# A pooled-attention and gated-MLP kernel on one core: its opening rebuilt

## The chip, the core and the metric

The kernel runs on one core of one Trainium2 chip. A core has five engines that run their own instruction queues and wait for each other through semaphores: PE (TensorE, matrix products into PSUM), DVE (VectorE), ACT (ScalarE), POOL (GpSimd) and SP (SyncE, which here only issues transfers). Transfers between main memory and the on-chip SBUF run on 16 DMA engines. The metric is the device time of one execution in microseconds (us).

## The reference

Eight batches of 576 positions; eight heads of 64. Keys and values are averaged over groups of 8 positions (72 pooled keys a head), then softmax attention, then a gated MLP whose gate mixes positions by the matrix `w_sg`.

```python
k_p = k.reshape(B, H, 72, 8, 64).mean(axis=3)          # the same for v_p
scores = 0.125 * q @ k_p.T                             # 576 x 72 for each head
attn = exp(scores - max); attn /= attn.sum() + 1e-9
x = concat_heads(attn @ v_p)                           # 8 x 576 x 512
h = gelu_tanh(x @ w_in)                                # w_in 512 x 1024
u, v = h[..., :512], h[..., 512:]
v_n = (v - mean) / sqrt(var + 1e-6) * g_ln
v_s = einsum('ts,bsd->btd', w_sg, v_n) + b_sg
out = x + (u * v_s) @ w_out                            # w_out 512 x 512
```

`w_in` and `w_out` arrive as 64-bit floats (4 MB and 2 MB), everything else as 32-bit floats.

## The kernel before

**Data.** A product in full precision is made of three products of rounded operands: every operand is split into a rounded part (`...h`, `...hi`) and a rest (`...l`, `...lo`), and high x high, high x low and low x high are summed in PSUM. For batch 0 alone (`WHOLE = (0,)`) the attention's value products run on unsplit 32-bit operands; each such product leaves two records on PE.

**Steps.** The work of one batch `b` is cut into steps, written as generators that advance piece by piece. A, B, C, E load keys, values, queries and the "left" rows (the last 8 of the 72 pooled rows of each head, kept apart); K pools the keys and writes the block-diagonal `kbd`; P pools the values; Q brings the queries of a head pair into `qT` (head dimension on partitions); S computes scores, their negated maximum `nmax`, the exponentials `e`, their sums `ssum`, and normalises; L and T transpose `e` (its left columns `el`, and the rest); V multiplies by the values and splits the result into `xhl`; H makes one row block of the value half of `w_in` (then gelu and the layer norm); U one column block of the other half; W multiplies by `w_sg`, gates; O multiplies by `w_out`; Z stores. Lower-case names are for weights: `lv0`, `lv1` load the two halves of `w_in`'s value columns, `lu0`, `lu1` the other columns, `lo0`, `lo1` `w_out`, `ls0` `w_sg`; `v0`..`v3`, `u0`..`u3`, `o0`..`o3` convert one piece of 128 x 512 numbers from 64 bits to two 32-bit parts (`step_w`); `s0`..`s4` transpose `w_sg`.

**Order.** Nothing is scheduled by a tool: two written tables set the order. `PROLOGUE` is the opening, a list of names such as `V0+0` (step V of head pair 0, batch 0) or `S0+1` (batch 1); each mention advances that step by one piece. `PERIOD` is repeated for each later batch. At the end every instruction is tied to the one before it on its engine, so each engine's queue runs exactly in the written order, and an instruction that waits holds all that stands behind it. All loads stand on SP's queue and share this rule: a load into a tile that is still being read waits, and so do the loads behind it.

**What the change touches.** In `load_q` the queries of every batch are loaded as 32-element runs, four transfers for a head pair, and `step_Q` turns them on DVE (L419). In `step_w`, ACT scales the high word (L198), DVE rebuilds sign and exponent (L201, L202) and takes the power of two apart (L203), ACT converts the low word to a number (L206) and rounds the high part (L207), POOL multiplies, subtracts and adds (L209, L219, L220). `BY_PSUM` makes the `v` pieces pass through PSUM. In `step_P`, batch 0's left values are scaled in place in the tile `left` (rows 64 to 96, L387); `step_V` multiplies those 32 rows (`lt[64:96]`) as a product of its own. `step_S` makes 10 exponentials a head pair (L453), each with its own bias and an accumulated sum. PSUM is used as two rings of two tiles, `mps` (MLP, weights and batch 0's scores) and `aps` (attention).

Of the kernel before, what the change touches and what calls it, by code (L numbers as in the profile page):

```python
# [35 lines left out]
O0+0 O1+0 S0+2 S1+2 O1+0 S2+2 O1+0 P2+2 V1+1 S2+2 C3+2 V3+1 S1+2 O2+0 O2+0 Z0+0 O2+0 V1+1 H2+1 S1+2 T0+2 S2+2
H2+1 S0+2 Q3+2 Z0+0 Z1+0
""".split()
PERIOD = """
# [11 lines left out]
def tile_pooled_attn_gmlp(ctx: ExitStack, tc: tile.TileContext, q, k, v, w_in, g_ln, w_sg, b_sg, w_out, out):  # L51
# [19 lines left out]
    BY_SUM = ()  # L71
# [79 lines left out]
    def load(o, i, queue=nc.sync):  # L151
        queue.dma_start(o, i)  # L152
# [593 lines left out]
```

## Time and profile before

| | us |
|---|---|
| median of the runs | 606.53 (603.07 to 606.60, 3 runs) |
| span of the profiled execution | 608.8 |
| PE's first product / first product of `w_sg` (step W) | 5.78 / 121.27 |
| one period of the repeated part | 66.0 |

For the profiled execution the record gives its span, 608.8 us, and no time of its own beside it; it is 2.3 us above the median of the runs. A row of a timeline reads: start, duration, engine, line, operation, output <- inputs, shape, how often in a row, and in brackets how long the engine had been idle and what ended it. The table by stretches gives for each engine its busy time and number of instructions, then PE's granted clock (1.00 is full speed), the busy share of the DMA engines and GB/s.

### The profile page before, as it was taken

How to read it: one execution, taken by the hardware profiler on the slowest of the kernel's cores; microseconds unless marked ns; L12 is line 12 of the kernel's file. 1: busy time of each engine (PE TensorE's matmuls, PEld its weight loads, DVE VectorE, ACT ScalarE, POOL GpSimd, SP SyncE). 2: the span in 40 equal slices, each digit the busy share in tenths (PEclk: the TensorE clock that was granted, in tenths of full speed). 3: DMA queues.
4: the chain of work that ended last, by engine and by line, in shares of the span. 5: the costliest groups of instructions: out<-in, count | busy, mean ns of one | idle time of the engine just before them, and what ended most of it. 6: DMA issues, size and time to landing. Idle time of an engine off the chain costs nothing.

```text
span 608.8 us, 10393 instructions
## 1 busy us (share of the span) xinstructions
PE 569.4 (94%) x3769; PEld 529.3 (87%) x3769; DVE 410.8 (67%) x566; ACT 360.8 (59%) x1091; POOL 235.5 (39%) x304
## 2 busy tenths in 40 slices
PE   3579569899999999999999999999999999999996
PEld 3564258899989998999999998999899999999996
DVE  1663698887785878667876878587866866434444
ACT  1685677957855677549754775567755975422310
POOL 2515756658240613253242523161324323242320
PEclk9575788999999999999999999999999999999999
DMA  7897460415325153413343162515341210112104
GB/s 173 185 271 199 101 165 4 88 36 95 59 55 110 36 106 64 92 36 79 54 92 75 37 112 55 110 36 102 67 92 19 40 21 1 20 25 34 20 1 78
DMA packets 166018, 46.33 MB, mean 76 GB/s; under 512 B 153488, under 2 KB 153488, under 8 KB 165968
## 3 DMA queue, kind: packets, MB, share of 16 engines
q1 hardware_dynamic: 161200, 45.10, 34.8%
q10 hardware_dynamic: 4768, 0.59, 0.6%
q8 instruction: 29, 0.48, 0.3%
q14 instruction: 21, 0.17, 0.1%
HBM read 36.23 MB, written 9.44 MB: 75 GB/s over the span
## 4 chain that ended last, share of the span: by engine, by line
PE 87%; ACT 5%; DVE 3%; DMA 2%; SPq 1%; issue 1%; POOL 0%; DVEq 0%; ACTq 0%; POOLq 0%
PE mps L97 68%; PE aps L97 13%; PE aps L134 4%; ACT e L453 3%; DMA raw<-in_moe_w_in 1%; SPq L152 1%; PE mps L242 1%; DVE top L202 1%; DMA left<-in_v 1%; DVE nmax L436 0%; DVE e L464 0%; PE aps L348 0%; DVE ssum L460 0%; ACT u L604 0%; POOL top L219 0%
## 5 line engine op out<-in xcount | busy, mean ns | idle before, releaser
L97 PE MATMUL mps<-wih,xhl 128*128 128x512 f32 x256 | 87.3, 407 | 4.6 <-ACT vg L567 4.6
L97 PE MATMUL mps<-xhl,wih 128*128 128x288 f32 x512 | 90.0, 298 | 0.7 <-DVE vg L563 0.7
L453 ACT ACTIVATE e<-aps,nmax 128x72 f32<-128x72 f32 x280 | 85.5, 353 | 4.1 <-DVE nmax L436 3.8
L629 POOL TENSOR_TENSOR glo<-u,ghi 128x576 fp32r<-128x576 f32 x32 | 45.3, 1427 | 108.1 <-ACT ghi L627 107.2
L97 PEld LDWEIGHTS mps<-xhl,wih 128*128 128x128 f32 x512 | 75.8, 189 | 2.4 <-DVE vg L563 1.0
L453 ACT ACTIVATION_READ_ACCUMULATOR e<-aps,nmax 128x1 f32 x280 | 66.8, 239 | 0.0
L97 PEld LDWEIGHTS mps<-wih,xhl 128*128 128x128 f32 x256 | 49.2, 192 | 16.1 <-ACT vg L567 5.0
L618 DVE SCALAR_TENSOR_TENSOR mps<-mps,gcol,bbc 128x576 f32<-128x576 f32 x32 | 26.4, 825 | 52.2 <-PE mps L97 52.2
L574 POOL TENSOR_TENSOR rstd<-mv,eps 128x1 f32<-128x1 f32 (+1 forms) x40 | 10.6, 264 | 117.4 <-DVE mv L572 107.9
L97 PE MATMUL mps<-wsh,vhh 128*128 128x288 f32 x256 | 55.7, 299 | 0.0
L97 PE MATMUL mps<-wsh,vhl 128*128 128x288 f32 x256 | 55.2, 297 | 0.0
L97 PE MATMUL mps<-xhl,wil 128*128 128x288 f32 x256 | 55.0, 296 | 0.0
L577 DVE TENSOR_SCALAR vg<-vg,mv,rstd 128x512 f32<-128x512 f32 (+1 forms) x40 | 41.6, 1041 | 19.8 <-POOL rstd L575 19.7
L97 PE MATMUL mps<-wsl,vhh 128*128 128x288 f32 x256 | 54.8, 295 | 0.0
L534 POOL TENSOR_TENSOR xhl<-x,xhl 128x576 fp32r<-128x576 f32 x32 | 45.3, 1430 | 22.4 <-ACT xhl L528 22.4
L97 PE MATMUL mps<-ghi,woh 128*128 128x288 f32 x240 | 52.6, 300 | 0.0
L97 PE MATMUL mps<-wil,xhl 128*128 128x512 f32 x128 | 51.5, 402 | 0.0
L97 PE MATMUL mps<-glo,woh 128*128 128x288 f32 x240 | 51.3, 295 | 0.0
L97 PE MATMUL mps<-ghi,wol 128*128 128x288 f32 x240 | 51.3, 295 | 0.0
L567 ACT ACTIVATE vg<-mps 128x512 f32<-128x512 f32 x32 | 19.0, 599 | 50.1 <-PE mps L97 49.9
L587 POOL TENSOR_TENSOR vhl<-vg,vhh 128x512 fp32r<-128x512 f32 x32 | 42.5, 1330 | 9.7 <-ACT vhh L585 9.6
L627 ACT CAST ghi<-u 128x576 fp32r<-128x576 f32 x32 | 21.5, 674 | 38.0 <-DVE u L620 38.0
(146 smaller groups left out, 1454.0 us busy)
## 6 DMA issues: line engine op xcount, KB each, us to landing
qraw<-in_q SPq DMA_DIRECT2D x128, 72.0 KB
out<-y SPq DMA_DIRECT2D x118, 72.0 KB
kvraw<-in_k SPq DMA_DIRECT2D x32, 256.0 KB
kvraw<-in_v SPq DMA_DIRECT2D x32, 256.0 KB
raw<-in_moe_w_in SPq DMA_DIRECT2D x4, 1024.0 KB
raw<-in_moe_w_out SPq DMA_DIRECT2D x2, 1024.0 KB
stage<-in_moe_w_sg SPq DMA_DIRECT2D x4, 288.0 KB
left<-in_k SPq DMA_DIRECT2D x16, 64.0 KB
```

The source lines that it names most:

```text
L97: nc.tensor.matmul(o, lhsT, rhs, start=start, stop=stop)
L134: nc.tensor.transpose(ps[:rows, i * P:(i + 1) * P], src(i), ident if i < NT - 1 else swap)
L152: queue.dma_start(o, i)
L453: nc.scalar.activation(e[:, i, h], slots[i][:, h], AF.Exp, bias=nmax[:, i, h:h + 1], **acc)
L534: nc.gpsimd.tensor_tensor(xhl[:, 1, g], x32[:, g], xhl[:, 0, g].bitcast(F32), op=ALU.subtract)
L567: nc.scalar.activation(vg, o, AF.Gelu_apprx_tanh)
L574: nc.gpsimd.tensor_tensor(rstd, mv[:, 1:2], eps[:n, 1:2], op=ALU.add)
L577: nc.vector.tensor_scalar(vg, vg, mv[:, 0:1], rstd, op0=ALU.subtract, op1=ALU.mult)
L587: (nc.gpsimd if i < NT - 1 else nc.vector).tensor_tensor(lo, vg, hi.bitcast(F32), op=ALU.subtract)
L618: nc.vector.scalar_tensor_tensor(vs, vs, gcol[:, d:d + 1], bbc.rearrange("p (a n) -> p a n", a=2), op0=ALU.mult, op1=ALU.add)
L627: nc.scalar.copy(ghi[:, d], uf)
L629: nc.gpsimd.tensor_tensor(glo[:, d], uf, ghi[:, d].bitcast(F32), op=ALU.subtract)
```

## The change

`PERIOD` is the same list with other line breaks. `PROLOGUE` is a new list with the same work, and these parts of the program are changed:

- **Queries of batch 0** (`NATURAL = (0,)`): two transfers a head pair with runs of 64 elements, into one large tile `early` (head pairs 0 to 2; it also takes batch 0's values) and a fourth buffer, so that no load of them waits for a reader. PE transposes them, six products of 128 x 96 a head pair, and ACT copies the result to `qT`.
- **Value products of batch 0**: `vl` and `lt` are tiles of their own with 96 rows, 64 of them zeroed at the start by POOL; step V multiplies all 96. `left` is no longer read by step V. `ah` alternates between two buffers.
- **Weights**: the low word, scaled, is added as an integer to the rebuilt high word (one POOL addition in place of a DVE mask, a POOL product and a POOL addition); rounding and rest follow. The pieces no longer pass through PSUM.
- **Softmax** of head pairs 1 and 3 of batch 0 and all four of batch 1 (`SOFTMAX`): DVE subtracts the maximum, ACT makes one exponential of 128 x 720, DVE sums.
- **Step H of batch 0**: all products with `xhl`'s high part first, the four with its low part last.
- **Loads of `w_in`'s value half** are issued on POOL's queue.

```diff
-    NATURAL = ()
+    NATURAL = (0,)
+    Q_ACT = (0, 1, 2, 3)
-    BY_PSUM = ("v",)
+    BY_PSUM = ()
-    SOFTMAX = {}
+    SOFTMAX = ((0, 1), (0, 3), (1, 0), (1, 1), (1, 2), (1, 3))
+    W_POOL = ("v",)
...
+    early = per.tile([P, 4 * POOL * D + 18 * P], F32, name="early", tag="xhl")
...
-        load(raw, sv)
+        load(raw, sv, nc.gpsimd if name in W_POOL else nc.sync)
...
             nc.scalar.activation(bits.bitcast(F32), high.bitcast(F32), AF.Copy, scale=2.0 ** -112)
-            yield
-            x = ring(per, shape, "vg", 3)
+            nc.scalar.activation(low, low.bitcast(U32), AF.Copy, scale=2.0 ** -29)
+            yield
             nc.vector.tensor_scalar(bits, bits, 3, None, op0=ALU.logical_shift_left)
             nc.vector.scalar_tensor_tensor(top, high, -0x80000000, bits, op0=ALU.bitwise_and, op1=ALU.bitwise_or)
-            nc.vector.tensor_scalar(x.bitcast(I32), top, -0x800000, None, op0=ALU.bitwise_and)
+            yield
+            nc.gpsimd.tensor_tensor(top, top, low, op=ALU.add)
+            yield
             top = top.bitcast(F32)
-            yield
-            nc.scalar.activation(low.bitcast(F32), low.bitcast(U32), AF.Copy, scale=2.0 ** -52)
             nc.scalar.copy(hi, top)
             yield
-            nc.gpsimd.tensor_tensor(x, x, low.bitcast(F32), op=ALU.mult)
...
-                nc.gpsimd.tensor_tensor(top, top, hi.bitcast(F32), op=ALU.subtract)
-                nc.gpsimd.tensor_tensor(lo, x, top, op=ALU.add)
+            (nc.vector if name in LO_W else nc.gpsimd).tensor_tensor(lo, top, hi.bitcast(F32), op=ALU.subtract)
...
+            for h in range(2):
+                load(t[:, :, h], q[b, 2 * g + h].rearrange("(t p) d -> p t d", t=6))
...
+        st["vl", b] = per.tile([96, 2, 4, D], F32, name="vl", tag="vl")
+        nc.gpsimd.memset(st["vl", b][0:64], 0.0)
+        for gp in range(2):
+            st["lt", b, gp] = per.tile([96, S], F32, name="lt", tag=f"lt{gp}")
+            nc.gpsimd.memset(st["lt", b, gp][0:64], 0.0)
...
+            ps = (mtile if g < 2 else atile)()
             for i in range(6):
+                nc.tensor.transpose(ps[:, i // 3, n * (i % 3):n * (i % 3 + 1)],
+                                    t[:, i].rearrange("p h d -> p (h d)"), ident[:n, :n])
+            yield
+            (nc.scalar.copy if g in Q_ACT else nc.vector.tensor_copy)(
+                qT.rearrange("p (a n) -> p a n", a=2), ps[:, :, 0:HALF])
...
-        mode = SOFTMAX.get(b, 0)
+        mode = 2 if (b, g) in SOFTMAX else 0
...
-                mm(o, vl[:, g // 2, gl:gl + 2], lt[64:96, sl], False, True)
+                mm(o, vl[:, g // 2, gl:gl + 2], lt[:, sl], False, True)
...
+        for c in range(KC if i < NT - 1 else 0):
+            mm(o, xhi[:, c, t], wih[:, c, sl], c == 0, False)
+            mm(o, xhi[:, c, t], wil[:, c, sl], False, False)
+            if b > 0:
+                mm(o, xlo[:, c, t], wih[:, c, sl], False, c == KC - 1)
         for c in range(KC):
             if i < NT - 1:
-                mm(o, xhi[:, c, t], wih[:, c, sl], c == 0, False)
-                mm(o, xhi[:, c, t], wil[:, c, sl], False, False)
-                mm(o, xlo[:, c, t], wih[:, c, sl], False, c == KC - 1)
+                if b == 0:
+                    mm(o, xlo[:, c, t], wih[:, c, sl], False, c == KC - 1)
```

**The loads on SP's queue**, from batch 0's last keys on. Before, as they stand in the queue (`kvraw`, `left`, `qraw` are keys and values, left rows and queries; `stage` is `w_sg`; `raw` are weights in 64 bits):

```order
L152 DMA stage<-in_moe_w_sg 64x576
L152 DMA bbc<-in_moe_b_sg 128x576
L152 DMA gcol<-in_moe_g_ln 128x4x1
L152 DMA qraw<-in_q 32x18x32 x4
L152 DMA raw<-in_moe_w_out 128x4x512
L152 DMA raw<-in_moe_w_in 128x4x512
L152 DMA kvraw<-in_k 64x2x512 x2
L152 DMA qraw<-in_q 32x18x32 x4
L152 DMA kvraw<-in_v 64x2x512 x2
L152 DMA raw<-in_moe_w_in 128x4x512
L152 DMA left<-in_k 32x1x512 x2
L152 DMA left<-in_v 32x1x512 x2
```

And now:

```order
L153 DMA stage<-in_moe_w_sg 64x576
L153 DMA bbc<-in_moe_b_sg 128x576
L153 DMA gcol<-in_moe_g_ln 128x4x1
L153 DMA kvraw<-in_k 64x2x512 x2
L153 DMA left<-in_k 32x1x512 x2
L153 DMA left<-in_v 32x1x512 x2
L153 DMA kvraw<-in_v 64x2x512 x2
L153 DMA raw<-in_moe_w_in 128x4x512
L153 DMA qraw<-in_q 32x18x32 x4
```

Batch 1's remaining keys and its left rows moved to directly behind `w_sg`, ahead of batch 1's values and queries and of three weight loads; the value half of `w_in` is gone from this queue.

**PE, the end of batch 0's attention**, from the second half of step V (`vb`, `ah`: values and transposed weights; `left`, `lt`: the left rows; `el`, `e`: exponentials; `kp`, `lp`: pooled keys). Before, with buffer numbers:

```order
L97 MATMUL aps_508<-ah_491,vb_106 128x288
L97 MATMUL aps_508<-lt_389,left_111 128x288
L242 MATMUL mps_520<-ident_70,stage_285 128x128
L242 MATMUL mps_520<-ident_70,stage_287 128x128
L242 MATMUL mps_520<-ident_70,stage_289 128x128
L242 MATMUL mps_520<-ident_70,stage_291 128x128
L242 MATMUL mps_520<-ident_70,stage_293 128x64
L348 MATMUL aps_540<-ident_70,kp_433 128x128 x2
L350 MATMUL aps_540<-ident_70,lp_93 128x128
L97 MATMUL aps_567<-kbd_84,qT_407 128x144 x5
L97 MATMUL aps_573<-kbd_84,qT_498 128x144 x5
L97 MATMUL mps_604<-wih_95,xhl_413 128x512
```

And now, from batch 1's keys on (each V step's two rows stand twice):

```order
L334 MATMUL aps_482<-ident_70,kp_304 128x128 x2
L336 MATMUL aps_482<-ident_70,lp_93 128x128
L99 MATMUL aps_500<-ah_466,vb_107 128x288
L99 MATMUL aps_500<-lt_113,vl_109 128x288
...
L99 MATMUL aps_511<-ah_475,vb_107 128x288
L99 MATMUL aps_511<-lt_113,vl_109 128x288
...
L99 MATMUL aps_518<-kbd_84,qT_488 128x144 x5
L99 MATMUL aps_545<-kbd_84,qT_506 128x144 x5
```

The key transposes of batch 1 moved from behind all four V steps to ahead of the last two, and two transposes of `w_sg` moved to ahead of the first; the first product of step H follows the last row here as it did before.

**ACT, the first rows of its queue.** Before (`kp`: pooled keys; `kbd`: their block-diagonal form; `raw`, `top`, `wih`: weight conversion):

```order
L338 COPY kp_116<-aps_117 128x128
L198 ACTIVATE mps_142<-raw_129 128x512
L338 COPY kp_116<-aps_132 128x128
L357 ACTIVATE kbd_84<-aps_151 64x4x64
L358 ACTIVATE kbd_84<-aps_151 64x4x8
L357 ACTIVATE kbd_84<-aps_151 64x4x64
L358 ACTIVATE kbd_84<-aps_151 64x4x8
```

And now:

```order
L324 COPY kp_118<-aps_119 128x128
L324 COPY kp_118<-aps_133 128x128
L343 ACTIVATE kbd_84<-aps_154 64x4x64
L344 ACTIVATE kbd_84<-aps_154 64x4x8
L343 ACTIVATE kbd_84<-aps_154 64x4x64
L344 ACTIVATE kbd_84<-aps_154 64x4x8
L406 COPY qT_158<-mps_159 128x576
L194 ACTIVATE top_186<-raw_147 128x512
L195 ACTIVATE raw_147<-raw_147 128x512
L194 ACTIVATE top_203<-raw_147 128x512
L195 ACTIVATE raw_147<-raw_147 128x512
L406 COPY qT_166<-mps_167 128x576
```

The first weight conversion, which waits for a load of 1 MB, moved from ahead of the second key copy to behind the keys and the first queries; the second query copy stands behind two conversions.

More of the change, by code (lines that the diff above doesn't have):

```diff
@@ L47 @@
+O1+0 Z1+0 Q3+2 S2+2 Z0+0 H2+1 S1+2 O2+0 S0+2 O2+0 T0+2 A0+3 C0+3 O2+0
 """.split()
@@ L261, in load_kv @@
         if b == 0 and which == 1:
-            if "kvraw0" not in st:
-                st["kvraw0"] = per.tile([P, 2, 2, POOL * D], F32, name="kvraw0", tag="xhl")
-            t = st["kvraw0"][:, gp]
+            t = early[:, 2 * gp * POOL * D:2 * (gp + 1) * POOL * D].rearrange("p (l r) -> p l r", l=2)
         else:
@@ L283, in load_q @@
         if b in NATURAL:
-            t = per.tile([S // 6, 2, 6, D], F32, name="qraw", tag=f"qraw{g % 2}")
-            load(t.rearrange("p h t d -> p h (t d)"),
-                 q[b, 2 * g:2 * g + 2].rearrange("h (p t) d -> p h (t d)", t=6))
+            if g < 3:
+                n = 4 * POOL * D + 6 * P * g
+                t = early[0:S // 6, n:n + 6 * P].rearrange("p (t h d) -> p t h d", t=6, h=2)
+            else:
+                t = dbl.tile([S // 6, 6, 2, D], F32, name="qraw", tag="x32")
+            for h in range(2):
+                load(t[:, :, h], q[b, 2 * g + h].rearrange("(t p) d -> p t d", t=6))
             st["q", b, g] = t
@@ L382, in step_P @@
         vlp = st.pop(("lp", b))[64:96]
-        v32 = st.pop(("left", b))[64:96, :, 0:4 * D].rearrange("p g (a d) -> p g a d", a=4)
+        left = st.pop(("left", b))
+        v32 = st["vl", b][64:96] if b in WHOLE else left[64:96, :, 0:4 * D].rearrange("p g (a d) -> p g a d", a=4)
         for h in range(2):
@@ L389, in step_P @@
         if b in WHOLE:
-            st["vl", b] = v32
             return
@@ L409, in step_Q @@
             n = S // 6
-            ps = atile()
+            ps = (mtile if g < 2 else atile)()
             for i in range(6):
-                for h in range(2):
-                    mm(ps[D * h:D * h + D, i // 3, n * (i % 3):n * (i % 3 + 1)], t[:, h, i], ident[:n, :n], True, True)
+                nc.tensor.transpose(ps[:, i // 3, n * (i % 3):n * (i % 3 + 1)],
+                                    t[:, i].rearrange("p h d -> p (h d)"), ident[:n, :n])
             yield
-            nc.vector.tensor_copy(qT.rearrange("p (t a i) -> p a i t", a=2, i=3),
-                                  ps[:, :, 0:HALF].rearrange("p a (i t) -> p a i t", i=3))
+            (nc.scalar.copy if g in Q_ACT else nc.vector.tensor_copy)(
+                qT.rearrange("p (a n) -> p a n", a=2), ps[:, :, 0:HALF])
             st["qT", b, g] = qT
@@ L480, in step_L @@
             if b in WHOLE:
-                lt = st["lt", b, gp] = per.tile([96, S], F32, name="lt", tag=f"lt{gp}")
-                nc.scalar.copy(lt[64:96], src)
+                nc.scalar.copy(st["lt", b, gp][64:96], src)
                 continue
```

69 lines of the change are left out of this document (28 added, 41 removed).

## The prediction

> **What bounds the kernel now.** I read the page's first part, then PE's busy time by stretches, then the timeline of the opening with the waits, then the clock in short stretches.
>
> ```profile
> span 608.8 us, 10393 instructions
> PE 569.4 (94%) x3769; PEld 529.3 (87%) x3769; DVE 410.8 (67%) x566; ACT 360.8 (59%) x1091; POOL 235.5 (39%) x304
> ```
> ```profile
> 0.00:41.50 41.50, 21.38 (x112) 19.84 (x112) 18.24 (x28) 19.88 (x96) 13.33 (x34) 0.78 0.83 196
> 41.50:66.70 25.20, 24.84 (x72) 13.41 (x72) 12.20 (x18) 15.59 (x28) 13.03 (x12) 0.62 0.60 178
> 66.70:78.70 12.00, 5.12 (x24) 4.45 (x24) 10.40 (x10) 6.25 (x14) 10.78 (x9) 0.57 0.69 161
> 78.70:121.50 42.80, 36.27 (x207) 31.07 (x207) 36.60 (x53) 35.60 (x119) 26.58 (x34) 0.92 0.34 81
> 121.50:190.00 68.50, 68.46 (x478) 65.14 (x477) 52.77 (x74) 48.26 (x142) 30.81 (x37) 1.00 0.35 70
> ```
>
> From 121.5 us on PE is busy without a gap at full clock (68.46 of 68.50 in the last row, and PE's 94% of the whole span). Neither `PERIOD` nor PE's work there is changed, so nothing can be won behind 121.5; what the opening saves moves the rest forward by as much. The opening has four stages: up to the left columns' transpose (L), the value products (V), a wait for batch 1, and H and U up to the first W. PE idles 20.1, 0.4, 6.9 and 6.5 us in them (stretch less busy), and its clock is 0.78, 0.62, 0.57 and 0.92 in the same order.
>
> The third stage's wait, in the SP queue's waits and in the timeline:
>
> ```profile
> SPq L152 <- PE aps L97: 14.0, 1, 14.0
> ```
> ```profile
> 65.93 1.40 SPq L152 DMA_DIRECT2D left<-in_k  x2
> ...
> 71.27 1.90 DVE L327 TENSOR_REDUCE lp<-left 64x128 f32<-64x1024 f32 x1 [1.45 <-DMA left<-in_v]
> ...
> 73.22 0.48 PE L350 MATMUL aps<-ident,lp 128*128 128x128 f32 x1 [3.26 <-DVE lp L327]
> ...
> 74.72 4.20 PE L97 MATMUL aps<-kbd,qT 128*128 128x144 f32 x20 [1.02 <-ACT kbd L358]
> ...
> 78.66 0.49 PE L97 MATMUL mps<-wih,xhl 128*128 128x512 f32 x1
> ```
>
> SP held batch 1's left rows for 14.0 us until the last V step had read the old ones; then load, sum, transpose, scores follow one after the other, and step H behind them on PE begins at 78.66.
>
> The value products and the clock:
>
> ```profile
> 46.28 1.32 PE L97 MATMUL aps<-lt,left 32*128 32x288 f32 x2
> 47.53 1.33 PE L97 MATMUL aps<-ah,vb 128*128 128x288 f32 x2
> ...
> 56.20 2.59 PE L242 MATMUL mps<-ident,stage 128*128 128x128 f32 x10
> ...
> 58.72 1.11 PE L134 MATMUL aps<-ident,e 128*128 128x128 f32 x4
> ...
> 63.07 0.75 PE L97 MATMUL aps<-ah,vb 128*128 128x288 f32 x2
> ...
> 65.79 0.44 PE L242 MATMUL mps<-ident,stage 128*128 128x128 f32 x2
> ```
> ```profile
> 29.90:33.30 3.40, 3.40 (x18) 3.39 (x17) 2.72 (x5) 3.40 (x25) 0.00 (x0) 0.50 1.04 299
> 33.30:36.70 3.40, 3.40 (x31) 3.40 (x31) 1.18 (x4) 1.97 (x11) 0.00 (x0) 0.98 1.06 356
> 36.70:40.10 3.40, 0.59 (x6) 0.40 (x4) 1.34 (x4) 3.40 (x21) 0.68 (x4) 1.00 1.13 180
> ...
> 50.30:53.70 3.40, 3.40 (x6) 1.25 (x6) 0.00 (x0) 1.51 (x3) 3.32 (x3) 0.50 0.86 201
> ...
> 57.20:60.60 3.40, 3.40 (x14) 2.28 (x13) 2.79 (x6) 2.27 (x4) 0.00 (x0) 0.50 0.03 12
> 60.60:66.70 6.10, 5.95 (x20) 2.62 (x19) 2.94 (x4) 4.29 (x8) 2.94 (x3) 0.99 0.01 3
> ```
>
> A 32-row product takes as long as a 128-row one (1.32, 1.33), yet the clock stays at 0.50 while V's products follow without a gap (50.3 to 53.7), and rises after 3.4 us of transposes (57.2 to 60.6), as it had after 3.4 us of 128-row work (29.9 to 33.3). Once up it survives V steps (60.6 to 66.7: 0.99); it had fallen with PE nearly idle from 36.7 on. At full clock a V step takes 65.79 - 63.07 = 2.7 us, at half about 5.
>
> **The change, part by part.** The sum is made against the span of 608.8; the result is then set from the median, 606.5.
>
> *Stage 1.*
>
> ```profile
> 8.41 1.88 DVE L327 TENSOR_REDUCE lp<-left 64x128 f32<-64x1024 f32 x1 [8.41 <-DMA left<-in_v]
> ...
> 14.95 0.62 ACT L198 ACTIVATE mps<-raw 128x512 f32<-128x512 f32 x1 [5.11 <-DMA raw<-in_moe_w_in]
> ...
> 18.31 2.74 PE L97 MATMUL mps<-kbd,qT 128*128 128x144 f32 x10 [2.06 <-DVE qT L419]
> ...
> 22.03 0.32 ACT L453 ACTIVATE e<-mps,nmax 128x72 f32<-128x72 f32 x1 [1.90 <-DVE nmax L436]
> ...
> 25.19 1.20 DVE L460 TENSOR_SCALAR ssum<-ssum 128x10 f32<-128x10 f32 x1 [1.79 <-ACT e L453]
> ...
> 41.71 1.06 PE L134 MATMUL aps<-ident,el 128*64 128x128 f32 x4 [4.42 <-POOL el L470]
> ```
> ```profile
> 7.12 13.01 SPq L152 DMA_DIRECT2D qraw<-in_q  x12
> ```
>
> ACT no longer stands at the load of 1 MB until 14.95 with the keys behind it. The left rows become the first limit: they are issued some 3.5 us later (two key loads and two query loads of 13.01 / 12 = 1.08 us ahead of them), so `lp` is done near 8.41 + 3.5 + 1.88 = 13.8 instead of 10.3, `kbd` near 15.3. PE then turns two head pairs of queries, about 1.3 us each (six transposes; four took 1.11 at 58.72), and ACT copies: first scores near 16.6, not 18.31. The exponentials of one head pair occupy ACT for 25.19 - 22.03 = 3.2 us; as one instruction of 720 numbers I estimate 0.85 (from 0.62 for 512), for two more DVE passes of about 0.9. The scores of pairs 2 and 3 still wait for PSUM tiles that pairs 0 and 1 hold until normalised, so only some of that arrives. I put L at 39.5: a gain of 2.2. Pooling the values and two `w_sg` transposes now stand in PE's queue ahead of L where it idled, so the clock should be up by then, as at 33.3.
>
> *Stages 2 and 3.* With the clock up, four V steps take 4 x 2.7 = 10.9; L, two transposes of `e`, two of `w_sg` and the keys of batch 1 are six groups of three to five transposes, about 0.8 each (two groups took 2.59 at half clock, at 56.20), 4.7; a wait for ACT's copy of `lt`, near L198's 0.62, 0.7: 16.3. The left rows of batch 1 no longer wait for step V: they stand behind 8.3 MB at most (keys, values and queries of batch 0 and keys of batch 1 at 1.18 each, `w_sg` and the bias 1.6, `w_in`'s value half 2.0), at stage 1's 196 GB/s 42 us, against a use near 50. So the third stage shrinks to the two score steps at full clock, 2.9 (4.20 at a clock partly half). H would begin at 39.5 + 16.3 + 2.9 = 58.7. ACT, with 15.59 us of work in stage 2 before, has hardly less in these 19 and stands in order; for its lag I add 2: 60.7, a gain of 18.0 on 78.66. Step H's low parts last hide POOL's last subtraction; nothing is counted for that.
>
> *Stage 4.*
>
> ```profile
> L209 POOL TENSOR_TENSOR vg<-vg,raw 128x512 f32<-128x512 f32 x10 | 13.5, 1346 | 26.6 <-ACT raw L206 26.6
> ```
> ```profile
> L327 DVE TENSOR_REDUCE kp<-kvraw 128x128 f32<-128x1024 f32 x2 | 4.0, 2020 | 0.0
> ...
> L436 DVE TENSOR_REDUCE nmax<-aps 128x10 f32<-128x720 f32 x4 | 3.6, 896 | 0.0
> ...
> L203 DVE TENSOR_SCALAR vg<-top 128x512 int32<-128x512 int32 x3 | 2.3, 752 | 0.2
> ...
> L488 DVE TENSOR_TENSOR lt<-aps,lt 32x576 fp32r<-32x576 f32 x2 | 1.5, 748 | 1.2 <-ACT lt L486 1.2
> ...
> L402 DVE TENSOR_TENSOR vl<-left,vl 32x512 fp32r<-32x512 f32 x1 | 0.9, 862 | 0.0
> ```
> ```profile
> 88.00:94.80 6.80, 5.71 (x15) 4.45 (x16) 5.19 (x10) 2.66 (x7) 2.69 (x5) 0.50 0.46 114
> ```
> ```profile
> 121.27 0.51 PE L97 MATMUL mps<-wsh,vhh 128*128 128x288 f32 x2
> ```
>
> Before, H to W takes 121.27 - 78.66 = 42.6, of which PE is idle 6.5 and half fast for 5.71. Now: DVE's 36.6, less four pooling sums that are done earlier or later (7.9: 4.0 for two), less L203 (2.3), less left-row work that moved behind W (1.5 and 0.9), plus 7.2 for four softmaxes (two more passes each, like `nmax`'s 0.9), plus three passes of weight work that moved in (2.2 by L203's 0.75): 33.4. PE's own work is about 31. So DVE and PE are level, and each will wait for the other: I add 3 for that, 2.9 for one more stretch at half clock as at 88.0 (half of 5.71), and 2.2 because a V step, a transpose and batch 2's keys now stand behind the first W: 41.5, a gain of 1.1. ACT loses 4 x 2.3 there and is no limit.
>
> *Rest.* The conversion drops one DVE pass and one POOL pass a piece (12 passes of 1.35, 16 us of POOL); POOL is busy 39% and hides it, and where it was late (stage 3) H no longer waits for it: nothing. Three memsets more on POOL stand ahead of its first load; what they cost is in the last rival. What a load costs on POOL's own queue no row shows; from below nothing (SP's issues are not counted as busy either), from above it holds POOL for as long as the same load took on SP, 14.95 - 6.5 = 8.4. POOL's first late user is `el` near 39; between 20 and 39 it has some 8 us of work, so I take nothing.
>
> Sum: 18.0 + 1.1 = 19.1 of 608.8, which leaves 589.7; set from the median, 606.5 - 19.1, about 587.5.
>
> **The transposes and the clock.** The 57.2 to 60.6 row shows the clock rising after a stretch in which 2.6 of 3.4 us or more were transposes. The Trainium skill, "TensorE: Matmul & The Clock Gate", section "Part 4: PE-mode transpose", says that transposes do not count as busy for the clock. By that rule the 24 new transposes would feed no rise and the opening would stay slow, at the time of the second rival; the row speaks against it here, though only one such stretch is on record.
>
> **The rivals.**
>
> *No slip (0.14).* If the 2, 3 and 2.9 that I added do not occur, the gain is 27: about 579.5. For it speaks that PE's order has no forced gap; against it, DVE at 36.60 of 42.80 in stage 4 already.
>
> *The clock stays at half through V (0.12).* 96 rows may count for as little as 32 did, the transposes that now fill the time ahead of V may count for little, and L may again come after an idle stretch as at 36.7 to 40.1. Then stage 2 keeps its 24 us: V costs 4 x 2.3 = 9 more, gain 10: 596.5.
>
> *The loads bind (0.10).* Stage 1's DMA share is 0.83 and above 1.00 between 29.9 and 40.1. If the opening moves 161 GB/s as in stage 3, 8.3 MB take 52 us, the keys of batch 1 come 5 late and `w_sg` as much, gain 9 to 14: about 596.
>
> *The value half of `w_in` comes late (0.14), which ends on the other side.* Its first load now follows POOL's memsets, and ACT's conversion of it stands ahead of the second query copy, DVE's ahead of the first maximum. Every microsecond that it lands after 16 delays the softmax chain by one. It landed at 14.95 from SP. At 35 the gain is gone; at 42 the kernel is over 1% slower, 613.5. For it speaks that no row shows such a load, against it that twice the 8.4 us still lands at 24 and leaves 11 of the gain. I give 0.08 to within 1% and 0.06 to slower.
>
> **How the numbers follow.** My forecast, 582 to 592, has 0.50 and names the time, 587.5. A measurement here tells 1%, about 6 us, from no change. The range reaches up to the half-clock and load cases, 601, and down to no slip, 578; outside are most of the late value half and the fastest corner, some 0.17. Faster: 0.50 + 0.14 + 0.12 + 0.10 = 0.86; same 0.08; slower 0.06.
>
> **What would show it.** First scores near 16.6 and L near 39.5; PE's clock 1.00 through all V steps; batch 1's left rows issued before 30 and no PE wait on `lp`; first H at 60.7 and first W near 100, with DVE busy over 85% between; from there the same dense rows. I am wrong if V runs at 0.50, if ACT's first conversion waits for its load beyond 18, or if PE waits on `wsl` or `lp`.

## The result and the profile after

The changed kernel takes 588.8 us (median of 4 runs, 588.5 to 589.1); the kernel before, run beside it, 604.8 us (601.9 to 606.6). The ratio is 0.974, with a 95% interval of 0.969 to 0.978: 2.6% faster. The prediction was 587.5, between 578 and 601. In every run the span of the profile is 1.6 to 2.0 us shorter than the time.

Busy time of each engine on the page of the changed kernel, whose profiled execution took 589.1 us:

```profile
span 587.4 us, 10314 instructions
...
PE 557.7 (95%) x3793; PEld 526.7 (90%) x3793; DVE 411.6 (70%) x562; ACT 349.3 (59%) x981; POOL 222.2 (38%) x297
```

The changed kernel by stretches, cut where its own stages end: the left columns' transpose (38.9), first H (57.3), first W (90.8), first O (120.0). The columns are those of the tables above: busy time of PE, PEld, DVE, ACT and POOL, the granted clock, the DMA share, GB/s.

```profile
0.00:38.90 38.90, 25.46 (x152) 24.00 (x153) 20.22 (x28) 20.48 (x67) 14.89 (x38) 0.87 0.96 226
38.90:57.30 18.40, 14.62 (x80) 11.16 (x80) 14.51 (x15) 14.59 (x28) 12.41 (x10) 1.00 0.94 196
57.30:90.80 33.50, 31.38 (x191) 27.23 (x189) 31.85 (x55) 26.30 (x43) 18.41 (x29) 1.00 0.58 129
90.80:120.00 29.20, 25.63 (x185) 25.18 (x183) 27.41 (x28) 17.23 (x32) 14.98 (x11) 0.94 0.32 67
120.00:190.00 70.00, 69.82 (x487) 66.39 (x486) 54.17 (x72) 46.85 (x146) 32.52 (x39) 1.00 0.38 76
```

Before, the stretch from first W to first O was dense, with PE busy throughout and the clock at 1.00:

```profile
121.30:143.10 21.80, 21.80 (x168) 21.65 (x167) 17.89 (x24) 13.88 (x27) 13.35 (x11) 1.00 0.29 62
```

| us from the start | before | after | moved by |
|---|---|---|---|
| left columns' transpose (L) | 41.71 | 38.87 | -2.8 |
| first H | 78.66 | 57.33 | -21.3 |
| first W | 121.27 | 90.80 | -30.5 |
| first O | 143.12 | 120.01 | -23.1 |

The third stage is gone, H to W is 9 us shorter, and then 7.4 us are given back between W and O (29.2 instead of 21.8). From O on both are dense, but from there to the end the changed kernel takes 467.4 us and the kernel before 465.7, so of the 23.1 us the span keeps 21.4.

The profiled execution before was a slow one: its span of 608.8 us belongs to a time of some 610.5 us, 4 and not 2.3 above the median of 606.5, at a mean granted clock of 0.954, where that kernel's runs beside the experiments took 599.8 to 609.4 us at 0.953 to 0.988. In the four traces with the old order (before, and b1, b2 and d1 below) the time from first O to the end is 465.7 to 466.0 us, so their spans differ ahead of O. By that, as an estimate, an execution at the median of 604.8 has its first O near 137.4, and the change moves it by some 17 us and not 23; which stage is shorter in such an execution no trace shows.

PE's timeline of the changed kernel shows the steps between (`aps<-lt,vl` is the product with the left rows, now 96 rows):

```profile
40.91 0.65 PE L99 MATMUL aps<-ah,vb 128*128 128x288 f32 x2
41.40 0.65 PE L99 MATMUL aps<-lt,vl 96*128 96x288 f32 x2
...
45.09 0.86 PE L227 MATMUL mps<-ident,stage 128*128 128x128 f32 x5 [1.09 <-DVE wsl L158]
...
48.00 0.27 PE L336 MATMUL aps<-ident,lp 128*128 128x128 f32 x1
...
56.12 1.46 PE L99 MATMUL aps<-kbd,qT 128*128 128x144 f32 x10 [2.45 <-DVE qT L410]
57.33 0.49 PE L99 MATMUL mps<-wih,xhl 128*128 128x512 f32 x1
...
98.65 0.37 PE L99 MATMUL aps<-ah,vbh 128*128 128x288 f32 x1 [3.33 <-DVE lt L478]
...
101.38 0.68 PE L99 MATMUL mps<-wsh,vhh 128*128 128x288 f32 x2
```

Products of V follow each other every 0.49 us for two records, so a V step of four such pairs takes 1.95 us. Batch 1's left rows (`lp`) cost PE no wait; a part of `w_sg` (`wsl`) cost it 1.1 us. The last two rows are where time is given back: a wait of 3.3 us, and the products of W behind it at half clock (0.68 us a row, where the same row takes 0.42 at full clock).

### The profile page after: what moved, and what is told of

Its sections match the earlier page's. It is cut to its first block, busy times and chain, and to the rows that moved or that the text cites. A ratio compares the mean times of both kernels' runs of the same rounds, so it can differ in the third digit from the quotient of the medians.

```text
span 587.4 us, 10314 instructions
## 1 busy us (share of the span) xinstructions
PE 557.7 (95%) x3793; PEld 526.7 (90%) x3793; DVE 411.6 (70%) x562; ACT 349.3 (59%) x981; POOL 222.2 (38%) x297
## 4 chain that ended last, share of the span: by engine, by line
PE 78%; DMA 8%; DVE 7%; SPq 3%; issue 1%; POOL 1%; ACT 0%; DVEq 0%
PE mps L99 65%; PE aps L99 10%; PE aps L133 3%; SPq L153 3%; DMA qraw<-in_q 2%; DMA left<-in_v 2%; DMA stage<-in_moe_w_sg 2%; DMA early<-in_q 2%; DMA kvraw<-in_k 1%; DVE kp L313 1%; DVE top L198 1%; DVE mps L612 1%; DVE qT L410 0%; DVE bst L565 0%; DVE u L614 0%
## 5 line engine op out<-in xcount | busy, mean ns | idle before, releaser
L623 POOL TENSOR_TENSOR glo<-u,ghi 128x576 fp32r<-128x576 f32 x32 | 45.2, 1425 | 112.1 <-ACT ghi L621 112.1
L99 PE MATMUL mps<-wih,xhl 128*128 128x512 f32 x256 | 85.7, 401 | 0.2
L444 ACT ACTIVATE e<-aps,nmax 128x72 f32<-128x72 f32 x240 | 73.3, 350 | 0.6 <-DVE nmax L427 0.3
L444 ACT ACTIVATION_READ_ACCUMULATOR e<-aps,nmax 128x1 f32 x240 | 56.6, 236 | 0.0
L571 DVE TENSOR_SCALAR vg<-vg,mv,rstd 128x512 f32<-128x512 f32 (+1 forms) x40 | 40.4, 1010 | 19.4 <-POOL rstd L569 19.3
L523 POOL TENSOR_TENSOR xhl<-x,xhl 128x576 fp32r<-128x576 f32 x32 | 45.3, 1429 | 21.9 <-ACT xhl L521 21.8
L561 ACT ACTIVATE vg<-mps 128x512 f32<-128x512 f32 x32 | 19.0, 597 | 47.2 <-PE mps L99 45.2
L621 ACT CAST ghi<-u 128x576 fp32r<-128x576 f32 x32 | 21.4, 672 | 37.7 <-DVE u L614 37.7
```

The lines of the kernel that those rows point to most:

```text
L99: nc.tensor.matmul(o, lhsT, rhs, start=start, stop=stop)
L444: nc.scalar.activation(e[:, i, h], slots[i][:, h], AF.Exp, bias=nmax[:, i, h:h + 1], **acc)
L523: (nc.vector if b in LO_DVE else nc.gpsimd).tensor_tensor(xhl[:, 1, g], x32[:, g], xhl[:, 0, g].bitcast(F32), op=ALU.subtract)
L561: nc.scalar.activation(vg, o, AF.Gelu_apprx_tanh)
L571: nc.vector.tensor_scalar(vg, vg, mv[:, 0:1], rstd, op0=ALU.subtract, op1=ALU.mult)
L621: nc.scalar.copy(ghi[:, d], uf)
```

## The experiments

Times are medians; ratios are to the kernel before, run on the same chip, with the 95% interval. These intervals are some 0.25 to 0.7% to either side, so a difference of under 2 us between two kernels is not resolved, and of under 4 us where the interval is widest (b3, b4).

| kernel | us | ratio |
|---|---|---|
| changed kernel | 588.8 | 0.974 (0.969 to 0.978) |
| a1: V with 32 rows | 591.0 | 0.983 (0.981 to 0.986) |
| a2: softmax on ACT | 597.1 | 0.992 (0.988 to 0.996) |
| a3: value half on SP | 587.5 | 0.977 (0.974 to 0.980) |
| b3: queries as before | 592.5 | 0.981 (0.974 to 0.988) |
| b4: conversion as before | 592.7 | 0.980 (0.973 to 0.987) |
| c3: H as before | 589.2 | 0.975 (0.970 to 0.980) |
| c1: second W ahead of V | 591.9 | 0.980 (0.975 to 0.984) |
| c2: c1, queries first, SP | 587.3 | 0.971 (0.967 to 0.976) |
| a4: new order, old operations | 619.3 | 1.029 (1.026 to 1.033) |
| d1: old order, new operations | 607.7 | 1.005 (1.002 to 1.009) |
| b1: before, own tile | 603.2 | 0.998 (0.993 to 1.003) |
| b2: before, own tile, 96 rows | 601.5 | 0.995 (0.991 to 0.998) |

### Order and operations, each alone

**a4, the new order with the operations of before**, and with the left values in a tile of their own (b1's diff, below).

```diff
-A0+0 E0+0 K0+0 A1+0 lv0 K0+0 K1+0 v0 K1+0 K2+0 C0+0
+A0+0 K0+0 A1+0 C0+0 K1+0 E0+0 lv0 K0+0 C1+0 K2+0 K1+0
...
-    BY_PSUM = ("v",)
+    BY_PSUM = ()
-            x = ring(per, shape, "vg", 3)
+            x = high.bitcast(F32)
-        ah = per.tile([P, S], F32 if b in WHOLE else F32R, name="ah")
+        ah = per.tile([P, S], F32 if b in WHOLE else F32R, name="ah", tag=("ah", "al")[g % 2] if b in WHOLE else "ah")
```

> The kernel before with its own operations and with three things changed: the new order of the opening, batch 0's left values in a tile of their own (without which that order cannot run), and transposed weights of batch 0 in two buffers. The mask of the weight conversion is kept in the raw tile and the v pieces do not pass through PSUM, as the order needs. Queries are transposed on DVE as before, V has 32 rows, ACT makes all exponentials, w_in's value half is on SP's queue, H is as before. Theory: the order and the free left tile carry most of the gain (third stage gone and clock up at V), the operations a part: 594 to 599 against about 604.8 before. Rival: the order alone is worth little without the lighter operations, since DVE and ACT are late for it: 602 to 608.

Both were too low: 619.3 us, 2.9% slower than before. PE's timeline of a4:

```profile
32.02 2.74 PE L97 MATMUL mps<-kbd,qT 128*128 128x144 f32 x10 [10.36 <-DVE e L466]
...
55.44 1.30 PE L242 MATMUL mps<-ident,stage 128*64 128x128 f32 x5 [2.55 <-DVE wsl L157]
...
58.47 1.32 PE L97 MATMUL aps<-lt,vl 32*128 32x288 f32 x2
...
66.01 1.32 PE L97 MATMUL aps<-lt,vl 32*128 32x288 f32 x2
...
72.06 0.65 PE L97 MATMUL mps<-wih,xhl 128*128 128x512 f32 x1
...
151.71 0.52 PE L97 MATMUL mps<-ghi,woh 128*128 128x288 f32 x2
```

The scores of the third head pair wait 10.4 us for a normalised `e`, which comes from the old string of exponentials; a later wait of 2.6 us is followed by the last two V steps at half clock (57.4 to 67.3). First H is at 72.1 and first W at 116.4, and so both are still earlier than in the kernel before (78.7 and 121.3). The loss comes behind W: first O is at 151.7, 35.3 us after first W, where the kernel before takes 21.9 and the changed kernel 29.2. PE waits there, and its clock is at 0.93 in a stretch of 48 us, of which it is busy 40.5.

```profile
120.00:168.00 48.00, 40.54 (x265) 38.37 (x265) 40.07 (x49) 31.63 (x99) 27.47 (x23) 0.93 0.38 81
```

**d1, the old order with the new operations** (all but the queries by PE).

```diff
-A0+0 K0+0 A1+0 C0+0 K1+0 E0+0 lv0 K0+0 C1+0 K2+0 K1+0
+A0+0 E0+0 K0+0 A1+0 lv0 K0+0 K1+0 v0 K1+0 K2+0 C0+0
...
-    NATURAL = (0,)
+    NATURAL = ()
```

> The old order of the opening with all new operations except the queries by PE (left values in a tile of their own, 96 rows in V, integer rounding of weights, softmax of six head pairs on DVE, H with its low part last, w_in's value half on POOL's queue; queries as before). Where a step has one piece more than before, the piece stands directly behind the one ahead of it. The run of the changed kernel with the old queries (592.5 us) differs from it in the order alone. Theory: the order is worth the rest of the third stage (DVE's key sums and the late left rows, H near 72 instead of 61) and little else, and it can only be used with the lighter operations: 597 to 602. Rival: the operations alone carry the gain, the order nothing: 590 to 594.

Both were too low again: 607.7 us, no better than before. In the old order DVE becomes the bound: from first H to first W it is busy 40.2 of 42.5 us, in b3 (below, the same operations in the new order) 31.5 of 33.1. The key and value sums of batches 1 and 2 stand there beside the new softmax passes (d1, 60 to 100 us; DVE busy 38.3 of 40, PE 29.7; in the kernel before 32.0 and 28.4):

```profile
60.00:100.00 40.00, 29.74 (x144) 24.22 (x144) 38.32 (x46) 23.58 (x44) 24.00 (x24) 0.87 0.41 101
```

The old list was not tuned again for the new operations, so a list near to it that does better is not excluded.

**b3, the changed kernel with the queries as before**, is d1's partner: the two differ in the order alone.

```diff
-    NATURAL = (0,)
+    NATURAL = ()
```

> The changed kernel with the queries of batch 0 loaded as before (32-element runs, four transfers a head pair into two buffers) and transposed by DVE instead of PE. Theory: this is one of the two lighter operations without which the new order failed (619 us with neither): the third query load waits for the first transpose on DVE and holds the loads behind it on SP, PE loses 24 products that filled its time ahead of V, and L comes 3 to 8 us later: 593 to 600. Rival: DVE and ACT only swap work, and the loads of the left rows and keys of batch 1 are far enough ahead: 588 to 590.

592.5 us, just under the theory's 593, with an interval that overlaps the changed kernel's. L comes at 45.75 instead of 38.87, but about half of that is won back: H at 60.94, W at 94.06. So with the new operations the order is worth 607.7 - 592.5 = 15.2 us (14.5 by the ratios); with the old ones, and with the small changes that it needs, it costs 619.3 - 603.2 = 16.1 us (19 by the ratios; a4 against b1). Neither half of the change gains anything alone.

### The left rows, the rows of V and the clock

**b1, before with the left values in a tile of their own.**

```diff
-        v32 = st.pop(("left", b))[64:96, :, 0:4 * D].rearrange("p g (a d) -> p g a d", a=4)
+        left = st.pop(("left", b))
+        v32 = (per.tile([96, 2, 4, D], F32, name="vl", tag="vl")[64:96] if b in WHOLE else
+               left[64:96, :, 0:4 * D].rearrange("p g (a d) -> p g a d", a=4))
```

> The kernel before with one thing changed: batch 0's left values go to a tile of their own (32 rows as before), so batch 1's left rows no longer wait for step V. Old order, all operations as before. Theory: SP's wait of 14.0 us goes, but DVE is next: the key sums of batch 1 stand ahead of the left sum on DVE until about 67 us, so first H moves from 78.7 to about 75 only: gain 1.5 to 4, time 598 to 601 against about 602 to 605 before. Rival: the load is all that the third stage waits for, and its 12 us shrink to about 4: gain 7 to 9.

603.2 us, no difference that can be told. The load no longer waits for V, but DVE's passes ahead of the left sum end at 71.1 and the sum begins at 71.09, where it was 71.27 (the trace is of b1's longest execution, 611.6 us, whose L came 1.2 us later). DVE's timeline of b1:

```profile
68.47 1.94 DVE L327 TENSOR_REDUCE kp<-kvraw 128x128 f32<-128x1024 f32 x1
70.32 0.74 DVE L250 TENSOR_TENSOR wtl<-mps,wth 64x576 fp32r<-64x576 f32 x1
71.09 1.90 DVE L327 TENSOR_REDUCE lp<-left 64x128 f32<-64x1024 f32 x1
```

The ratio leaves room for a gain of up to 4 us, so the theory's 1.5 to 4 is not excluded; the rival's 7 to 9 is.

**b2, the same with 96 rows in V.**

```diff
-                lt = st["lt", b, gp] = per.tile([96, S], F32, name="lt", tag=f"lt{gp}")
-                nc.scalar.copy(lt[64:96], src)
+                nc.scalar.copy(st["lt", b, gp][64:96], src)
...
-                mm(o, vl[:, g // 2, gl:gl + 2], lt[64:96, sl], False, True)
+                mm(o, vl[:, g // 2, gl:gl + 2], lt[:, sl], False, True)
```

> The same as the run with the own tile alone, and V of batch 0 multiplies 96 rows of vl and lt (64 of them zeroed at the start). Theory: 96 rows let the clock rise within the first V step, which 32 rows never did (8 products in a row at half in the fresh order run, too), and their weight loads overlap: V's first two steps take 2 to 3 us each instead of 5 and the stage from 41.5 to 66.7 us becomes 5 to 7 shorter than with the own tile alone; 3 to 6 us less than that run in all. Rival: rows do nothing for the clock, the first two V steps stay at 0.50 and only the weight loads overlap: within 2 us of that run.

601.5 us, 1.8 below b1, which is less than expected and not resolved; what the trace shows of the clock is plain. The clock of b2 by stretches:

```profile
44.00:46.00 2.00, 2.00 (x5) 1.35 (x4) 1.77 (x4) 1.21 (x3) 1.80 (x2) 0.50 1.05 403
46.00:48.00 2.00, 1.79 (x6) 1.09 (x5) 1.89 (x2) 1.25 (x3) 1.92 (x2) 0.84 1.06 391
48.00:50.00 2.00, 2.00 (x12) 1.60 (x11) 0.00 (x0) 1.97 (x4) 2.00 (x3) 1.00 1.11 238
```

V's first product, at 43.6, is at half clock as it was before; the clock is up 3 us later, within V's first step. With 32 rows it had stayed at 0.50 through two whole steps, in the kernel before and again in a4 (10 us without a gap, 57.4 to 67.3; it rose there only after another 5 us of 128-row scores). In b2 the clock had fallen just ahead of V, at 43.3, and not at L as before. But in d1, with the old order and 96 rows, it was down from L (43.9) on as before, and it rose within V's first step too, which begins at 47.4 (d1, PE's timeline):

```profile
48.34 0.93 PE L99 MATMUL aps<-lt,vl 96*128 96x288 f32 x2
49.10 0.65 PE L99 MATMUL aps<-ah,vb 128*128 128x288 f32 x2
```

V ends at 56.9 in b2. But PE now waits for DVE's key sums and for the left rows' load, and first H comes at 74.2, 4.5 earlier than in the trace before (b2, PE's timeline):

```profile
61.67 0.66 PE L348 MATMUL aps<-ident,kp 128*128 128x128 f32 x2 [2.94 <-DVE kp L327]
68.14 0.48 PE L350 MATMUL aps<-ident,lp 128*128 128x128 f32 x1 [5.82 <-DVE lp L327]
```

b2's ten times lie between 601.0 and 603.1 us, b1's ten between 601.0 and 611.6. So against b1's shortest executions 96 rows gain nothing, and against its longest 8.6 us; no trace shows the clock of a short execution with 32 rows in the old order.

**a1, the changed kernel with 32 rows in V.**

```diff
-                mm(o, vl[:, g // 2, gl:gl + 2], lt[:, sl], False, True)
+                mm(o, vl[64:96, g // 2, gl:gl + 2], lt[64:96, sl], False, True)
```

> The changed kernel (588.8 us) with one thing undone: step V of batch 0 multiplies 32 rows again (rows 64 to 96 of vl and lt), in their own tiles and in the new order. Theory: the new order lets PE arrive at V with its clock up, and a 32-row product costs only its weight load, which is not overlapped (pairs at 0.68 us instead of 0.49 at full clock). So V's four steps take 10.9 us instead of 7.8 at a clock of 1.00 throughout, and the time is 591 to 593. Rival: the 96 rows keep the clock up; with 32 rows the clock falls to 0.50 within the V steps as it was before, a V step takes about 5 us, and the time is 598 to 602.

591.0 us, the theory's lower end, though not in the theory's place. The clock is 1.00 through V, as it said, and the products are further apart, 0.68 us instead of 0.49. The weight loads of a1 and then of the changed kernel (engine PEld):

```profile
43.63 0.30 PEld L99 LDWEIGHTS aps<-ah,vb 128*128 128x128 f32 x2 [0.39 <-issue]
44.32 0.29 PEld L99 LDWEIGHTS aps<-lt,vl 32*128 32x128 f32 x2 [0.39 <-issue]
```
```profile
41.16 0.43 PEld L99 LDWEIGHTS aps<-lt,vl 96*128 96x128 f32 x2
41.65 0.43 PEld L99 LDWEIGHTS aps<-ah,vb 128*128 128x128 f32 x2
```

With 32 rows each pair of loads begins 0.39 us after the last one, about when the product ahead has ended; with 96 rows they follow without a gap, beside the products. So 32 rows hold a clock that is up (also in a4's first two steps, 45.1 to 50.8), with 96 rows one that is down has risen (b2, d1), and here the order has it up already.

That the loads cost a1 its 2.2 us the trace does not show. From L to first H a1 takes 17.0 us and the changed kernel 18.5: its longer products fill the two waits for DVE (1.1 and 2.45 us), which it no longer has. It is behind at L already, by 2.6 us, as PE waits 6.5 us for batch 0's `lp` instead of 1.3, long before V (a1, PE's timeline):

```profile
18.67 0.45 PE L336 MATMUL aps<-ident,lp 128*128 128x128 f32 x1 [6.47 <-DVE lp L313]
...
41.51 0.63 PE L133 MATMUL aps<-ident,el 128*64 128x128 f32 x4
...
56.08 2.72 PE L99 MATMUL aps<-kbd,qT 128*128 128x144 f32 x20
```

What the 96 rows are worth in the new order stays open.

### The other parts, undone one by one

**a2, softmax on ACT again.**

```diff
-    SOFTMAX = ((0, 1), (0, 3), (1, 0), (1, 1), (1, 2), (1, 3))
+    SOFTMAX = ()
```

> The changed kernel with the softmax of the six head pairs back on ACT (ten exponentials of 72 each with their own sum, no DVE subtraction and no DVE sum). Theory: stage 4 ran level with DVE and ACT once the queries and conversions had been lightened, and ACT is the engine that stood in order; each head pair gives ACT 2.4 us back and takes 1.8 us from DVE. In the opening ACT then delays the left columns' transpose by 2 to 5 us, and H to W becomes 36 to 40 us instead of 33.5: 593 to 598. Rival: DVE bounds the stage from 57 to 91 us (37.0 of 40 us busy between 60 and 100), so giving DVE 7 us back in it makes the kernel faster: 584 to 587.

597.1 us: the theory, with L at 42.2, and with more than its 36 to 40 us from first H to first W (a2):

```profile
57.95:99.30 41.35, 34.33 (x191) 29.44 (x189) 27.33 (x48) 35.68 (x121) 21.44 (x31) 0.92 0.44 104
```

The stage is 7.9 us longer than in the changed kernel (57.30:90.80 above), with ACT at 35.7 of 41.4 us and the clock at 0.92. In the changed kernel DVE takes ACT's place, at 31.9 of 33.5, but has less to do than ACT had here.

**a3, the value half on SP's queue.**

```diff
-    W_POOL = ("v",)
+    W_POOL = ()
```

> The changed kernel with the value half of w_in loaded on SP's queue again, in the same place of the order (first load behind the left rows, ahead of the queries). Theory: the opening is bound by the bytes that all DMA engines move (0.96 busy in the first 40 us), so the queue does not matter beyond its place in line: 1 MB in SP's order ahead of the query loads delays the first queries by some 3 us but comes itself earlier; L at 39 to 42, time 588 to 592. Rival one: the queue makes nothing (within 1 us of 588.8). Rival two: GpSimd's issue (0.7 to 0.9 us of POOL each) and late landing cost time, so that SP is better: 585 to 587.

587.5 us, nothing that can be told. The trace has first scores at 16.0 instead of 17.5 and H at 53.9 instead of 57.3, in an execution of 585.5 us, the shortest of a3's four. No gain of POOL's queue is shown.

**b4, the old conversion** of the eight pieces of `w_in`, as a branch of its own:

```diff
+            if name in "vu":
+                nc.scalar.activation(low.bitcast(F32), low.bitcast(U32), AF.Copy, scale=2.0 ** -52)
...
+                x = high.bitcast(F32)
...
+                nc.vector.tensor_scalar(x.bitcast(I32), top, -0x800000, None, op0=ALU.bitwise_and)
...
+                nc.gpsimd.tensor_tensor(x, x, low.bitcast(F32), op=ALU.mult)
...
+                nc.gpsimd.tensor_tensor(top, top, hi.bitcast(F32), op=ALU.subtract)
+                nc.gpsimd.tensor_tensor(lo, x, top, op=ALU.add)
+                return
```

> The changed kernel with the old arithmetic in the conversion of the eight w_in pieces (a third DVE pass, three POOL passes instead of two; the mask is kept in the raw tile). Theory of the prediction: POOL and DVE hide it but for DVE's part of the opening (4 passes before L, 4 behind V), 589 to 592. Rival: conversion is the work that holds DVE and POOL back where the new order failed with the old operations (619 us): POOL carries el and the products one after the other, so L is 4 us or more later and the time is 594 or more.

592.7 us, between the two, with an interval that overlaps the changed kernel's. In its trace L is at 38.0 and H at 55.6, earlier than in the changed kernel, and W at 91.9 later. Up to first H nothing of it is seen. H to W takes 36.3 us in it instead of 33.5; whether that is the conversion's price, which the prediction put at nothing, stays open.

**c3, step H as before.** Its products take high and low parts in turn for batch 0 too.

```diff
-            if b > 0:
+            if True:
                 mm(o, xlo[:, c, t], wih[:, c, sl], False, c == KC - 1)
...
-                if b == 0:
+                if False:
```

> The changed kernel with step H of batch 0 as before (high and low products in turn). Theory of the prediction: POOL's last subtraction of xhl is done before H begins, so nothing changes: 588 to 589.5. Rival: H's first row block waits for it, 1 to 2 us: 590 to 591.

589.2 us: nothing, as expected.

### The time given back behind W

**c1, the second step W ahead of batch 1's first V.**

```diff
-T1+1 V0+1 T1+1 o0 W0+0
+T1+1 W0+0 V0+1 T1+1 o0
```

> The changed kernel with one step moved on PE: the second step W stands ahead of batch 1's first step V instead of behind it. Theory: PE's wait of 3.3 us for the left weights ahead of V (98.65) and the half clock behind it (99.5 to 103) are the part of the gain that is given back; W's products fill both, 3 to 5 us: 584 to 586. Rival: the work behind is bound by DVE (9.8 of 10 us busy there), and the wait only moves: 588 to 589.

591.9 us, no faster and rather slower. PE waits as long at the same place, now for ACT (c1, PE's timeline):

```profile
98.08 0.66 PE L99 MATMUL mps<-wsh,vhh 128*128 128x288 f32 x2 [3.12 <-ACT u L598]
```

and ACT had been waiting for DVE (c1, ACT's timeline):

```profile
96.09 0.63 ACT L475 CAST lt<-aps 32x576 fp32r<-32x576 f32 x1 [4.11 <-DVE lt L478]
...
97.38 0.65 ACT L598 ACTIVATE u<-mps 128x576 f32<-128x576 f32 x1
```

The gelu that frees W's PSUM tile stands behind the copies of `lt`, which wait for DVE's passes on `lt`. Both steps hang on one DVE queue, whose rows ahead of the first pass on `lt` (95.67) are these in the changed kernel:

```profile
90.56 1.66 DVE L198 SCALAR_TENSOR_TENSOR top<-raw,top 128x512 int32<-128x512 int32 x1
92.25 1.68 DVE L581 TENSOR_TENSOR vht<-vg,vht 64x512 fp32r<-64x512 f32 x1
93.96 1.68 DVE L393 TENSOR_TENSOR vl<-left,vl 32x512 fp32r<-32x512 f32 x1
...
100.58 0.69 DVE L198 SCALAR_TENSOR_TENSOR top<-raw,top 128x512 int32<-128x512 int32 x1
...
105.84 1.80 DVE L198 SCALAR_TENSOR_TENSOR top<-raw,top 128x512 int32<-128x512 int32 x1
```

The first three are 2.8 us longer than the same passes elsewhere (0.69 for L198 at 100.58; 0.69 and 0.86 for the other two before). POOL has two passes of 1.6 us and one of 1.75 from 90.21 to 95.1, and one beside the last row:

```profile
90.21 3.17 POOL L581 TENSOR_TENSOR vhl<-vg,vhh 128x512 fp32r<-128x512 f32 x2
93.35 1.75 POOL L200 TENSOR_TENSOR top<-top,raw 128x512 int32<-128x512 int32 x1
...
105.81 1.27 POOL L205 TENSOR_TENSOR wol<-top,woh 128x512 fp32r<-128x512 f32 x1 [3.16 <-ACT woh L203]
```

The Trainium skill, "SBUF — State Buffer", section "Who interferes with whom", says that a DVE instruction with two inputs in SBUF contends with a GpSimd instruction that reads SBUF. The three rows have two such inputs and fit it. So do the other L198 passes of this trace: the two beside a POOL pass on 128x512 take 1.66 and 1.80 us, the other ten 0.69 to 0.74. No kernel was run with those POOL passes elsewhere, so that they cause the wait of 3.3 us is argued and not shown.

**c2, c1 with all queries of batch 0 loaded first and the value half on SP's queue.**

```diff
-B0+0 C2+0 K2+0 A1+1 Q0+0 v1 v1 v1 S0+0 C3+0 S0+0
+C2+0 C3+0 B0+0 K2+0 A1+1 Q0+0 v1 v1 v1 S0+0 S0+0
-    W_POOL = ("v",)
+    W_POOL = ()
```

> The same with two more changes: all query loads of batch 0 ahead of batch 1's first keys and batch 0's values, and w_in's value half on SP's queue (1.2 us better by itself). Theory: PE's waits for the queries of the third and the fourth head pair (2.3 and 2.9 us) fall away, L is 1 to 3 us earlier than with the SP queue alone (36.7), and the time is 581 to 584. Rival: the values, which come later instead, make PE wait ahead of V by as much: 584 to 586.

587.3 us, not told apart from the changed kernel or a3, against an expected 581 to 584. L is at 36.3, where a3 has 36.7. The waits for queries turned into waits for `e`, 3.7 us in two (c2, PE's waits from 10 to 40 us: engine, line, what it waited for, total, times, longest):

```profile
PE mps L99 <- DVE e L455: 3.7, 2, 2.7
...
PE mps L403 <- DMA early<-in_q: 1.2, 1, 1.2
```

Behind the queries the softmax chain was PE's next wait, and no version was found that beats the changed kernel by more than can be measured.

## Why the prediction was right

**Stage 1** was put at 2.2 us and gave 2.8. First scores came at 17.5, not 16.6, as PE waited 2.3 us for the second pair's queries, and the softmax chain behind them made up for it: with the softmax on ACT L is at 42.2 (a2).

**Stages 2 and 3.** First H was put 18.0 us earlier and came 21.3 earlier; without stage 1's part, 15.8 and 18.5. The mechanism is as predicted: the clock is 1.00 through V, and PE does not wait for `lp`. Batch 1's left rows were issued at 31.3, where 30 had been named. The largest miss of the sum are the four V steps, put at 10.9: at 1.95 us each they are 7.8, as 32-row products had been paying for their weight loads at full clock too (a1). This alone did not bring H forward, though: a1, whose steps take 10.9, gets from L to first H in 17.0 us, so that PE's terms and its waits do not simply add up there. The waits were put too small and on the wrong engine: 0.7 and 2 us had been added for ACT, and PE waited 3.8 us, nearly all for DVE (1.1 and 2.45 us). The first of these is for `wsl`, which the prediction had named as a sign of being wrong; it cost 1.1 us and moved no conclusion.

**Stage 4** was put at 41.5 and took 33.5, and first W came at 90.8, where 100 had been named. DVE was to be the limit with 33.4 us and had 31.9. What the sum had added to that for waits (3), half clock (2.9) and moved work (2.2) is missing there, and about as much appears behind W: 7.4 us more between W and O, made of 3.6 us idle and 3.8 us more busy time; if the moved work is the 2.2 of the sum, the rest is half clock. From H to O the prediction has 41.5 + 21.8 = 63.3, the trace 62.7. That they agree so closely is luck: the terms were estimates for another place, and the wait behind W is not one that the prediction had seen. The step that fell is the sentence that nothing changes behind 121.5: it held for PE's own work from O on, to within 1.7 us, not for the stretch from W to O, where DVE and ACT were late in the new order. It stood beside the term of 2.2 us for work moved behind W, which speaks against it already.

**Sum.** 19.1 was forecast on the span of 608.8; the span fell by 21.4. The medians fell by 16.0, because the profiled execution before took longer than its median and the one after did not; on the medians the forecast gain was 3 us too large. The time came out nearer, 588.8 against 587.5, as the median of 606.5 that the sum was set from became 604.8 with one more run.

**No part stands alone, which the prediction does not say.** The old operations in the new order lose 16 us and the new operations in the old order gain nothing, as a4 and d1 show. The prediction did not meet that, as it priced each stage with all edits in it. Undone one at a time, softmax on DVE is worth 8 to 11 us (by the medians and by the ratios), the 96 rows 2 to 6, though a1's trace does not place that in V; the queries on PE and the conversion are worth some 4 each, not resolved, and the queue and step H nothing. With the old operations left in, neither of the two orders shows a gain.

**Clock and transposes.** The rule that the prediction takes from the Trainium skill ("TensorE: Matmul & The Clock Gate", section "Part 4: PE-mode transpose"), that transposes do not count as busy, had one row against it. b1 adds a second: its clock rises at 62, after 4.8 us of transposes (56.3 to 61.1) and 1 us of V's 128-row products (0.8 us of them stand at the end of the prediction's row, too). But 3.5 us of transposes ahead of V had raised nothing, in b1 (42.9 to 46.4) or before (41.7 to 45.2), so how much they count stays open. In the changed kernel the work ahead of V was mixed, so it tells nothing more.

**The rivals.** None came about as a whole, but parts of two did: H to W had little slip (PE idle 2.1 of 33.5 us), and loads did hold PE. DMA engines were busy 96% of the first 38.9 us, and PE waited for queries twice, 2.3 and 2.9 us, but neither the keys nor the left rows of batch 1 came late for it. The value half on POOL's queue was there at 16.2, within the bounds named (ACT's timeline of the changed kernel):

```profile
16.21 0.66 ACT L194 ACTIVATE top<-raw 128x512 f32<-128x512 f32 x1 [0.40 <-DMA raw<-in_moe_w_in]
```

## What to carry to other kernels

An order written by hand is tuned to the lengths of its operations. Here the lighter operations gained nothing in the old order, and the new order lost with the old operations, so the two are to be tried together and priced by stage. When a wait is taken away, look for what is next in the same engine's queue: here a load that no longer waited gained nothing, since DVE's sums stood ahead of its use. A wait that two steps share (PE's for the left weights behind W) was not filled by exchanging the two. And when a part is undone, look where its trace loses the time: a1's total fitted its theory, and its loss lay in front of the part.

## What was not expected of the hardware

- Products of 32 rows held the clock where it was: 10 us of them, in turn with 128-row ones and without a gap, stayed at 0.50 (a4), and at 1.00 they kept it (a1, and a4's first two steps). With 64 rows of zeros added, the clock rose within 3 us (b2, d1).
- At full clock a pair of 32-row products took 0.68 us and a pair of 96-row products 0.49, since the 32-row weights were not loaded beside the product ahead (a1). A V step is 1.95 us instead of 2.7.
- One exponential of 720 numbers takes 0.80 to 0.85 us on ACT, ten of 72 with sums 3.1.
- A load of 1 MB on POOL's queue held POOL for 0.7 to 0.9 us and landed after 10.0, with the DMA engines busy 96%.
